# Attention with keys on partitions, no row maximum and v stationary, followed by the same SwiGLU with its weight tiles read again from DRAM

## The chip, the cores and the metric

One core of one Trainium2 chip runs the kernel. It has five engines with instruction queues of their own: TensorE (PE in the profile; its weight loads are listed as PEld), VectorE (DVE), ScalarE (ACT), GpSimd (POOL) and SyncE (SP), which here issues most DMAs. The metric is the device time of one execution in microseconds, lower is better. Three runs of the kernel before took 2514.51, 2516.18 and 2516.25 us; the median is 2516.18.

## The reference

Attention over 8 sequences and 12 heads, 448 tokens and 64 features a head, with q and k divided by their root mean square; then a SwiGLU block on the joined heads.

```
q, k, v: (8, 12, 448, 64) float32; g_q, g_k: (64,) float32
q_n, k_n = q / rms(q) * g_q, k / rms(k) * g_k      # rms over the 64 features
scores = q_n @ k_n^T / 8
attn   = exp(scores - max) / (sum(exp(scores - max)) + 1e-9)
x      = (attn @ v) as (3584 tokens, 768)
xn     = x / rms(x) * rms_g                        # over the 768 features
g, val = xn @ w_gate, xn @ w_val                   # 768 -> 1536
out    = (g * sigmoid(g) * val) @ w_out            # 1536 -> 768
```

The three weight matrices arrive as float64 and everything is computed in float32. The gains are `g = abs(randn(64)) + 0.5`; with the seed of the reference the largest absolute product g_q * g_k of one feature is 5.26. A vector of 64 features divided by its root mean square has length 8.

## The kernel before, in words

A sequence of 448 tokens is cut into four chunks of 112, and heads are taken in pairs: head 0 of a pair has its 64 features on partitions 0 to 63, head 1 on 64 to 127. There are 8 x 6 = 48 pairs, and the unit of attention is one chunk of 112 queries of one head, `(g, j, t)`: pair, head in the pair, chunk. There are 48 units a sequence.

For each pair, `norm_pair` (lines 132 to 149) divides q and k by their root mean square on GpSimd and VectorE, and `turn_pair` (lines 151 to 163) transposes both on TensorE so that features lie on partitions. `score` (L171) then gives 112 queries on partitions against all 448 keys; VectorE takes the row maximum (L173), ScalarE the exponential with the row sum (L175). `turn_e` (L181) transposes that tile in four pieces, copied out by VectorE and ScalarE in turn, because `values` (L194) needs keys on partitions: for each unit four matmuls with a transposed piece of e as the stationary operand and 64 columns of v streaming. After a pair the result is divided by the row sums (L204). Tokens lie on partitions, so after a sequence `norm_x` reduces along the row, and `turn_x` (L226) transposes x into `xT`, features on partitions.

The FFN of a sequence is 24 projections of six matmuls (`project`, L237; gate and value in turn over 12 blocks of 128 hidden features), a Tanh on ScalarE and two products on VectorE, which write `hT`; then eight output blocks of 112 tokens by 384 features, twelve matmuls each (`project_out`, L259). A float32 matmul is two passes, two MATMUL records in the trace.

The weights stay on chip as float32 for the whole kernel. `load_weight` (lines 86 to 110) reads a piece of float64 as pairs of 32-bit words and rounds it with four passes on VectorE, three on GpSimd and one on ScalarE. 60 pieces (36 of 512 columns, 24 of 384) are spread over the 48 units of the first sequence.

The order of work is written out in the loop at the end: at each unit a score, the weight pieces that are due, the transposes of the unit before, FFN items of the previous sequence in proportion to their cost, and the values of the unit before that. The first sequence has no FFN under it, and the FFN of the last has no attention over it. A scheduler arranges each engine's queue from this, so an engine's own order can differ a little from the program's.

Of the kernel before, what the change touches and what calls it, by code (L numbers as in the profile page):

```python
# [8 lines left out]
F32 = mybir.dt.float32  # L9
I32 = mybir.dt.int32  # L10
U32 = mybir.dt.uint32
I64 = mybir.dt.int64
ALU = mybir.AluOpType
ACT = mybir.ActivationFunctionType
AX_X = mybir.AxisListType.X
PSUM = bass.MemoryType.PSUM

B, H, S, D = 8, 12, 448, 64
DM, DF = H * D, 1536
NT, P = 4, 112  # a sequence is 4 chunks of 112 tokens; token p * 4 + t lies on partition p  # L20
# [3 lines left out]
CW = 512  # columns of a float64 weight chunk  # L24
# [3 lines left out]
def kernel(  # L28
# [12 lines left out]
):  # L41
    nc = tc.nc
# [41 lines left out]
    def load_weight(dst, src):  # L84
        """dst [128, n] float32; src [128, n] float32, or the bits of float64 as int64."""
# [15 lines left out]
        # 2^exponent with the sign, as float32 bits: 0 below float32's range, infinity above it.  # L101
# [4 lines left out]
        # The significand: its upper 21 bits exactly, then rounded with the lower 32.  # L106
# [25 lines left out]
    def norm_pair(g):  # L132
        """q and k over their root mean squares, as [token, (q k), chunk, head, d]."""
# [17 lines left out]
    def turn_pair(g):  # L151
        """Both transposed, d on partitions (64 for each head), times g_q / 8 and g_k."""
# [12 lines left out]
    def score(g, j, t):  # L165
        """Softmax numerators of 112 queries against all keys, and their sum."""
# [73 lines left out]
    def gate(b, fc):  # L240
        """2 * silu(g) = g * (1 + tanh(g / 2))"""
        project(b, fc, wg, "g")
        g = st.pop(("g", b, fc))
        th = th_pool.tile([128, S], F32, name="th")
        nc.scalar.activation(th, g, ACT.Tanh, scale=0.5)  # L245
        ga = st["ga", b, fc] = ga_pool.tile([128, S], F32, name="ga")
        nc.vector.scalar_tensor_tensor(ga, th, 1.0, g, ALU.add, ALU.mult)  # L247
# [78 lines left out]

# [28 lines left out]
```

## Time and profile before

| | |
|---|---|
| median of 3 runs | 2516.18 us (2514.51 to 2516.25) |
| profiled execution, span from first to last instruction | 2514.6 us |
| instructions | 24315 |
| TensorE matmul busy | 2406.5 us, 96% |
| TensorE weight loads | 1406.0 us, 56% |
| VectorE | 811.8 us, 32% |
| ScalarE | 532.8 us, 21% |
| GpSimd | 523.6 us, 21% |
| DMA | 73.92 MB, mean 29 GB/s |

The profiled execution is known by its span; the median of the timed runs is 1.6 us above it. Matmuls overlap in the array and the ends in their records are modelled, so the duration of a record is longer than the distance to the next start; weight loads run beside matmuls and are listed as an engine of their own. The page cuts the span into 40 slices of 63 us: in the first four TensorE is busy for 5 to 8 tenths, from the sixth on for 9 tenths and more in all but one, while VectorE and GpSimd have 5 to 8 tenths in the first four and 1 to 3 from the seventh on.

### The profile page before, as it was taken

What the parts mean: (1) busy time and instruction counts of PE and PEld (TensorE: products, weight loads), DVE (VectorE), ACT (ScalarE), POOL (GpSimd) and SP (SyncE); (2) the same over time, 40 slices, a digit from 0 to 9 for tenths busy, and PEclk for the clock granted to TensorE, in tenths of its full rate; (3) what the DMA queues carried; (4) which work ended last, traced back from release to release, by engine and by line L of the source; (5) the groups of instructions that cost most, each with busy time, mean ns of one, the idle gap of its engine ahead of it and who ended that gap; (6) DMA issues with size and microseconds to landing.
All of it is one profiled execution on the core that took longest, in us unless ns stands there. A gap on an engine that the chain in (4) does not pass through costs nothing.

```text
span 2514.6 us, 24315 instructions
## 1 busy us (share of the span) xinstructions
PE 2406.5 (96%) x9792; PEld 1406.0 (56%) x9792; DVE 811.8 (32%) x1337; ACT 532.8 (21%) x1285; POOL 523.6 (21%) x443
## 2 busy tenths in 40 slices
PE   5778899999999999999999999999999999999899
PEld 3445555555555555555555655555555565556455
DVE  5868733223322232222322233222332232221110
ACT  2223322212212122212212122222222122121100
POOL 7777612112111111111211211111121121110000
PEclk9999999999999999999999999999999999999999
DMA  4333200000000100000000000001000010000000
GB/s 125 123 119 108 85 12 19 15 22 24 18 15 17 30 21 11 19 26 22 19 12 14 28 25 15 12 25 32 11 19 15 22 30 12 8 6 11 6 1 22
DMA packets 48511, 73.92 MB, mean 29 GB/s; under 512 B 4880, under 2 KB 37136, under 8 KB 48400
## 3 DMA queue, kind: packets, MB, share of 16 engines
q1 hardware_dynamic: 47296, 72.37, 9.7%
q8 instruction: 78, 1.28, 0.2%
q14 instruction: 33, 0.27, 0.0%
q10 hardware_dynamic: 1104, 0.00, 0.0%
HBM read 61.35 MB, written 11.01 MB: 29 GB/s over the span
## 4 chain that ended last, share of the span: by engine, by line
PE 86%; POOL 6%; DVE 3%; issue 2%; ACT 2%; DMA 0%; POOLq 0%; ACTq 0%; SPq 0%; DVEq 0%
PE ff L237 35%; PE ff L259 20%; PE sc L171 12%; PE av L194 10%; PE tr L181 7%; PE tr L158 2%; PE tr L226 2%; POOL arena L103 1%; POOL arena L104 1%; ACT junk L214 1%; POOL rs L143 1%; DVE arena L109 1%; DVE arena L105 1%; POOL wg L110 1%; POOL qn L146 1%
## 5 line engine op out<-in xcount | busy, mean ns | idle before, releaser
L259 PE MATMUL ff<-wo,hT 128*112 128x384 f32 x1536 | 505.0, 486 | 0.0
L237 PE MATMUL ff<-xT,wg 128*128 128x448 f32 x1152 | 464.0, 549 | 0.0
L194 PEld LDWEIGHTS av<-vt,eT 112*112 112x112 f32 x3072 | 384.7, 194 | 133.5 <-issue 65.9
L237 PE MATMUL ff<-xT,wv 128*128 128x448 f32 x1152 | 452.5, 540 | 0.0
L171 PE MATMUL sc<-qkT 64*112 64x448 f32 x768 | 427.9, 646 | 8.8 <-ACT e L175 5.3
L194 PE MATMUL av<-vt,eT 112*112 112x64 f32 x3072 | 386.8, 275 | 26.3 <-DVE eT L184 12.7
L173 DVE TENSOR_REDUCE top<-sc 112x1 f32<-112x448 f32 x384 | 238.2, 622 | 483.7 <-PE sc L171 483.7
L137 POOL TENSOR_TENSOR qn<-qk 112x1024 f32<-112x1024 f32 x48 | 92.0, 1917 | 1424.1 <-issue 1313.0
L259 PEld LDWEIGHTS ff<-wo,hT 128*112 128x112 f32 x1536 | 267.2, 177 | 207.2 <-issue 0.4
L175 ACT ACTIVATE e<-sc,top 112x448 f32<-112x448 f32 x384 | 243.8, 635 | 500.9 <-DVE top L173 485.2
L237 PEld LDWEIGHTS ff<-xT,wv 128*128 128x128 f32 x1152 | 211.2, 190 | 177.6 <-issue 177.6
L237 PEld LDWEIGHTS ff<-xT,wg 128*128 128x128 f32 x1152 | 213.2, 193 | 171.7 <-issue 171.7
L181 PEld LDWEIGHTS tr<-ident,e 112*112 112x112 f32 x1536 | 164.6, 144 | 250.6 <-issue 149.8
L181 PE MATMUL tr<-ident,e 112*112 112x112 f32 x1536 | 246.7, 288 | 14.9 <-ACT e L175 14.9
L186 ACT COPY eT<-tr 112x448 f32<-112x448 f32 x192 | 101.9, 530 | 472.1 <-PE tr L181 472.1
L247 DVE SCALAR_TENSOR_TENSOR ga<-th,ff 128x448 f32<-128x448 f32 x96 | 59.6, 621 | 406.7 <-ACT th L245 406.7
L253 DVE SCALAR_TENSOR_TENSOR hT<-ga,ff 128x448 f32<-128x448 f32 x96 | 59.6, 621 | 337.4 <-PE ff L237 337.4
L171 PEld LDWEIGHTS sc<-qkT 64*112 64x112 f32 x768 | 113.1, 187 | 52.9 <-issue 18.9
L143 POOL TENSOR_TENSOR rs<-ms,mhalf 112x16 f32<-112x16 f32 x48 | 141.8, 2954 | 4.0
L245 ACT ACTIVATE th<-ff 128x448 f32<-128x448 f32 x96 | 52.1, 543 | 391.9 <-PE ff L237 391.9
L184 DVE COPY eT<-tr 112x448 f32<-112x448 f32 x192 | 118.2, 616 | 4.7 <-PE tr L181 4.3
L267 DVE COPY y<-ff 112x384 f32<-112x384 f32 x32 | 17.8, 558 | 272.6 <-PE ff L259 272.6
(40 smaller groups left out, 1021.5 us busy)
## 6 DMA issues: line engine op xcount, KB each, us to landing
qk<-in_q_dram SPq DMA_DIRECT2D x48, 224.0 KB, 2.9
qk<-in_k_dram SPq DMA_DIRECT2D x48, 224.0 KB, 3.2
vt<-in_v_dram SPq DMA_DIRECT2D x48, 224.0 KB, 2.6
out_dram<-y SPq DMA_DIRECT2D x32, 336.0 KB, 2.7
arena<-in_moe_w_gate_dram SPq DMA_DIRECT2D x18, 512.0 KB, 3.6
arena<-in_moe_w_val_dram SPq DMA_DIRECT2D x18, 512.0 KB, 3.6
arena<-in_moe_w_out_dram SPq DMA_DIRECT2D x24, 384.0 KB, 3.1
gq<-in_g_q_dram ACTq DMA_DIRECT2D x2, 0.2 KB, 3.3
```

The source lines that it names most:

```text
L137: nc.gpsimd.tensor_tensor(qn.rearrange("p a t h d -> p (a t h d)"), qk.rearrange("p a h x -> p (a h x)"), qk.rearrange("p a h x -> p (a h ...
L143: nc.gpsimd.tensor_tensor(rs, ms, mhalf[0:P, :], ALU.pow)
L171: nc.tensor.matmul(ps, lhsT=qkT[r, 0, t * P:(t + 1) * P], rhs=qkT[r, 1, :], start=True, stop=True)
L173: nc.vector.tensor_reduce(out=top, in_=ps, axis=AX_X, op=ALU.max, negate=True)
L175: nc.scalar.activation(e, ps, ACT.Exp, bias=top[:, 0:1], accum_out=st["den", g][:, j, t:t + 1])
L181: nc.tensor.transpose(ps[0:P, c, :], e[:, c * P:(c + 1) * P], ident[0:P, 0:P])
L184: nc.vector.tensor_copy(eT, ps[0:P])
L186: nc.scalar.copy(eT, ps[0:P])
L194: nc.tensor.matmul(av[:, j, t, :], lhsT=eT[:, c, :], rhs=vt[:, j, c, :], start=(c == 0), stop=(c == NT - 1))
L237: nc.tensor.matmul(ps, lhsT=w[:, c, fc * 128:(fc + 1) * 128], rhs=st["xT", b][:, c, :], start=(c == 0), stop=(c == NDC - 1))
L247: nc.vector.scalar_tensor_tensor(ga, th, 1.0, g, ALU.add, ALU.mult)
L259: nc.tensor.matmul(ps, lhsT=st["hT", b][:, fc, t * P:(t + 1) * P], rhs=wo[:, fc, n * HALF:(n + 1) * HALF], start=(fc == 0), stop=(fc == NF ...
```

## The change

The kernel before is kept whole as `any_scores`. A new program `safe_scores` comes first; it also sets a flag on the chip, and `any_scores` runs after it, behind a branch, where the flag is set. The flag is 8 times the largest absolute g_q * g_k against 80, the bound on a score from the lengths of the normed vectors.

In the new program the scores have keys on partitions: `score` takes a chunk of 112 keys as the stationary operand and streams all 448 queries. There is no maximum; the exponential takes the key's inverse root mean square as its per-partition scale, so k is transposed as it was loaded. The tile of exponentials can stream straight into `values`, where v is stationary (64 columns) and the result has features on partitions, head 0 on 0 to 63 and head 1 on 64 to 127. The sum over keys is six additions on GpSimd and one matmul per head with ones. x comes out as `xT`; its norm is a matmul with ones and one that spreads the result over partitions.

The weights of gate and value are held in three tiles of one block each. In the first FFN they are rounded from float64 and stored as float32 in DRAM; later sequences read them from there, three blocks ahead. `W_AHEAD` is that 3. `wo` stays on chip and is rounded block by block in the first FFN. Output blocks are 128 tokens instead of 112: six for an even sequence, whose last 64 tokens go with the next one's, and eight for an odd one. `fill` puts in FFN items of the sequence before; two of them (`LEFT`) are kept for the steps of the norm of x.

```
+    raw_pool, cv_pool = pool("c_raw", 2), pool("c_cv", 2)
...
+    nc.vector.tensor_scalar(flag, top, 8.0, SAFE, ALU.mult, ALU.is_gt)
...
+    def convert(dst, src):
+        if src.dtype == F32:
+            nc.sync.dma_start(out=dst, in_=src)
+            return
+        a, n = src.shape[1], src.shape[2]
+        assert a * n == DM
+        raw = raw_pool.tile([128, 2 * DM], I32, name="raw")
+        nc.sync.dma_start(out=raw.rearrange("p (a n w) -> p a (n w)", a=a, w=2).bitcast(I64), in_=src)
+        words = raw.rearrange("p (n w) -> p n w", w=2)
+        lo, hi = words[:, :, 0], words[:, :, 1]
+        top = cv_pool.tile([128, DM], I32, name="top")
+        nc.scalar.activation(top.bitcast(F32), hi.bitcast(F32), ACT.Abs)
+        nc.gpsimd.tensor_scalar(top.bitcast(F32), top.bitcast(F32), 122879.9921875, 2.0**-15, ALU.min, ALU.max)
+        nc.vector.tensor_scalar(top, top, 3, 0x3FFFFFF8, ALU.logical_shift_left, ALU.bitwise_and)
+        nc.vector.scalar_tensor_tensor(top, hi, -(2**30), top, ALU.bitwise_and, ALU.bitwise_or)
+        power = cv_pool.tile([128, DM], I32, name="power")
+        nc.vector.tensor_scalar(power, top, -(2**23), None, ALU.bitwise_and)
+        low = cv_pool.tile([128, DM], F32, name="low")
+        nc.vector.scalar_tensor_tensor(low, lo.bitcast(U32), 2.0**-52, power.bitcast(F32), ALU.mult, ALU.mult)
+        nc.gpsimd.tensor_tensor(dst.rearrange("p a n -> p (a n)"), top.bitcast(F32), low, ALU.add)
+    def weight(w, n):
...
+        if b == 0:
+            convert(t, src[:, fc * 128:(fc + 1) * 128].rearrange("(c p) f -> p c f", p=128))
+            nc.sync.dma_start(out=kept[w][fc], in_=t.rearrange("p c f -> p (c f)"))
+        else:
+            nc.sync.dma_start(out=t.rearrange("p c f -> p (c f)"), in_=kept[w][fc])
...
+    def score(g, cs):
+        for c in cs:
+            for j in range(2):
+                r = slice(j * D, (j + 1) * D)
+                ps = sc[c, j] = ps_s.tile([P, S], F32, name="sc")
+                nc.tensor.matmul(ps, lhsT=qkT[r, 1, c * P:(c + 1) * P], rhs=qkT[r, 0, :], start=True, stop=True)
+        for (c, j), ps in sc.items():
...
+            nc.scalar.activation(e, ps, ACT.Exp, scale=rs[:, n:n + 1])
+        for j in range(2):
...
+                    nc.gpsimd.tensor_tensor(es, es, st["e", g, c, j], ALU.add)
+    def values(g):
+        for c in range(NT):
+            for j in range(2):
+                nc.tensor.matmul(av[j * D:(j + 1) * D, 0:S], lhsT=vt[:, j, c, :], rhs=st["e", g, c, j],
+                                 start=(c == 0), stop=(c == NT - 1))
+        for j in range(2):
+            nc.tensor.matmul(den[j * D:(j + 1) * D, 0:S], lhsT=ones[0:P, :], rhs=st["es", g, j], start=True, stop=True)
...
+    def val(b, fc):
+        project(b, fc, "v")
...
+        weight("v", b * NFC + fc + W_AHEAD)
+        if b == 0:
+            weight_out(fc)
...
+    for g in range(NG):
...
+        load_pair(g + 2)
+        norm_pair(g + 1)
+        score(g, (0, 1))
+        fill()
+        score(g, (2, 3))
+        fill()
+        turn_pair(g + 1)
+        fill()
+        values(g)
+        divide(g)
+        fill()
+        if hp == NPAIR - 1:
+            fill(len(todo) - LEFT)
+            rms_x(b)
+            fill(1)
+            norm_x(b)
+            fill(1)
...
+    safe_scores(tc, *args, flag)
+    large = nc.values_load(flag[0:1, 0:1], min_val=0, max_val=1)
+    with tc.If(large > 0):
+        any_scores(tc, *args)
```

How the instructions of TensorE move in a steady stretch is seen from its queue. Before, inside the second sequence (`ff` are projections, `sc` scores, `tr` transposes, `av` values):

```order
L171 MATMUL sc<-qkT 112x448
L181 MATMUL tr<-ident,e 112x112 x4
L237 MATMUL ff<-xT,wg 128x448 x6
L194 MATMUL av<-vt,eT 112x64 x4
L171 MATMUL sc<-qkT 112x448
L181 MATMUL tr<-ident,e 112x112 x4
L194 MATMUL av<-vt,eT 112x64 x4
L171 MATMUL sc<-qkT 112x448
L181 MATMUL tr<-ident,e 112x112 x4
L237 MATMUL ff<-xT,wv 128x448 x6
```

After, at the same depth, with `den` the sums over keys:

```order
L500 MATMUL sc<-qkT 112x448 x4
L575 MATMUL ff<-xT,wg 128x448 x6
L500 MATMUL sc<-qkT 112x448 x4
L575 MATMUL ff<-xT,wv 128x448 x6
L575 MATMUL ff<-xT,wg 128x448 x6
L485 MATMUL tr<-ident,qn 128x112 x4
L485 MATMUL tr<-ident,qk 128x112 x4
L575 MATMUL ff<-xT,wv 128x448 x6
L520 MATMUL av<-e,vt 64x448 x8
L524 MATMUL den<-es,ones 64x448 x2
L575 MATMUL ff<-xT,wg 128x448 x6
```

Each short chain of value, score and transposes between two projections has given way to longer blocks, four scores or eight values and two sums at a time; the transposes left are those of q and k.

At the end of the first sequence TensorE's queue read before:

```order
L181 MATMUL tr<-ident,e 112x112 x4
L171 MATMUL sc<-qkT 112x448
L181 MATMUL tr<-ident,e 112x112 x4
L171 MATMUL sc<-qkT 112x448
L194 MATMUL av<-vt,eT 112x64 x8
L171 MATMUL sc<-qkT 112x448 x3
L226 MATMUL tr<-ident,x 128x112 x16
L237 MATMUL ff<-xT,wg 128x448
```

And now, with `msx` and `rb` the two small steps of the norm of x:

```order
L500 MATMUL sc<-qkT 112x448 x8
L485 MATMUL tr<-ident,qn 128x112 x4
L485 MATMUL tr<-ident,qk 128x112 x4
L520 MATMUL av<-e,vt 64x448 x8
L524 MATMUL den<-es,ones 64x448 x2
L500 MATMUL sc<-qkT 112x448 x8
L555 MATMUL msx<-ones,ss 112x1 x4
L565 MATMUL rb<-ident,rs_789 128x112 x4
L485 MATMUL tr<-ident,qn 128x112 x4
L575 MATMUL ff<-xT,wg 128x448 x6
```

The transposes of x between the first projections are gone; scores of the next pair stand ahead of the norm, and a whole pair's work has no projection in it.

VectorE's queue holds the rounding of weights. In the first sequence before (`arena` are its pieces):

```order
L105 SCALAR_TENSOR_TENSOR arena<-arena 128x512
L109 SCALAR_TENSOR_TENSOR arena<-arena 128x512
L102 TENSOR_SCALAR arena<-arena 128x512
L107 TENSOR_SCALAR arena<-arena 128x512
L184 COPY eT<-tr 112x448
L173 TENSOR_REDUCE top<-sc 112x1
L105 SCALAR_TENSOR_TENSOR arena<-arena 128x512
L109 SCALAR_TENSOR_TENSOR arena<-arena 128x512
```

And in the second sequence now, where `ga` and `hT` are the gating products of the FFN:

```order
L417 SCALAR_TENSOR_TENSOR top<-raw,top 128x768
L420 TENSOR_SCALAR power<-top 128x768
L422 SCALAR_TENSOR_TENSOR low<-raw,power 128x768
L590 SCALAR_TENSOR_TENSOR hT<-ga,ff 128x448
L416 TENSOR_SCALAR top<-top 128x768
L417 SCALAR_TENSOR_TENSOR top<-raw,top 128x768
L420 TENSOR_SCALAR power<-top 128x768
L422 SCALAR_TENSOR_TENSOR low<-raw,power 128x768
L584 SCALAR_TENSOR_TENSOR ga<-th,ff 128x448
L490 COPY qkT<-tr 128x448
```

The rounding stood between the maxima and copies of attention; it now stands between the two products that the projections' PSUM banks wait for.

## Rows read from the trace of the kernel before

**Rows 1.** The page's engine line (busy us, share, instructions) and chain by line.
```profile
PE 2406.5 (96%) x9792; PEld 1406.0 (56%) x9792; DVE 811.8 (32%) x1337; ACT 532.8 (21%) x1285; POOL 523.6 (21%) x443
...
PE ff L237 35%; PE ff L259 20%; PE sc L171 12%; PE av L194 10%; PE tr L181 7%; PE tr L158 2%; PE tr L226 2%; POOL arena L103 1%; POOL arena L104 1%; ACT junk L214 1%; POOL rs L143 1%; DVE arena L109 1%; DVE arena L105 1%; POOL wg L110 1%; POOL qn L146 1%
```

**Rows 2.** Timeline of TensorE, steady stretch: start us, us, engine, line, operation, tiles.
```profile
...
1509.55 0.91 PE L194 MATMUL av<-vt,eT 112*112 112x64 f32 x8
1510.39 1.00 PE L171 MATMUL sc<-qkT 64*112 64x448 f32 x2
1511.32 0.59 PE L181 MATMUL tr<-ident,e 112*112 112x112 f32 x4
1511.75 0.91 PE L194 MATMUL av<-vt,eT 112*112 112x64 f32 x8
1512.59 1.00 PE L171 MATMUL sc<-qkT 64*112 64x448 f32 x2
...
```

**Rows 3.** The chain in order of time: start us, us, what; the FFN.
```profile
499.07 7.74 PE ff L259 x24
...
2340.85 107.50 PE ff L237 x286
2448.36 61.93 PE ff L259 x192
```

**Rows 4.** Stretches: length, busy per engine, granted clock, DMA share, GB/s; start, seam, inside.
```profile
20.00:310.00 290.00, 228.33 (x762) 141.20 (x763) 219.34 (x344) 88.68 (x201) 222.70 (x214) 1.00 0.37 110
597.00:608.00 11.00, 9.15 (x41) 5.10 (x41) 5.85 (x11) 6.42 (x16) 1.21 (x2) 0.78 0.08 22
620.00:880.00 260.00, 260.00 (x1098) 151.14 (x1098) 70.44 (x118) 50.78 (x126) 41.12 (x30) 1.00 0.07 20
```

**Rows 5.** Timeline of TensorE in the first sequence, columns as in rows 2.
```profile
36.65 1.62 PE L194 MATMUL av<-vt,eT 112*112 112x64 f32 x8
38.19 1.83 PE L171 MATMUL sc<-qkT 64*112 64x448 f32 x2
```

**Rows 6.** Timeline of TensorE at two seams: two adjacent scores of different heads.
```profile
598.43 1.34 PE L171 MATMUL sc<-qkT 64*112 64x448 f32 x4
...
2042.96 1.34 PE L171 MATMUL sc<-qkT 64*112 64x448 f32 x4
```

**Rows 7.** Groups by line (busy us, mean ns, idle before): normalization and exponentials.
```profile
L175 ACT ACTIVATE e<-sc,top 112x448 f32<-112x448 f32 x384 | 243.8, 635 | 500.9 <-DVE top L173 485.2 <-PE tr L181 15.4
L143 POOL TENSOR_TENSOR rs<-ms,mhalf 112x16 f32<-112x16 f32 x48 | 141.8, 2954 | 4.0
L146 POOL TENSOR_TENSOR qn<-qk,rs 112x512 f32<-112x512 f32 x96 | 98.1, 1042 | 3.8
L137 POOL TENSOR_TENSOR qn<-qk 112x1024 f32<-112x1024 f32 x48 | 92.0, 1917 | 1424.1 <-issue 1313.0 <-PE tr L158 107.5 <-DMA qk<-in_k_dram 3.6
```

**Rows 8.** Groups by line: VectorE's passes of a weight conversion, 512 columns wide.
```profile
L105 DVE SCALAR_TENSOR_TENSOR arena<-arena 128x512 int32<-128x512 int32 x36 | 41.3, 1149 | 47.6 <-POOL arena L104 46.9
L109 DVE SCALAR_TENSOR_TENSOR arena<-arena 128x512 f32<-128x512 uint32 x36 | 26.1, 726 | 0.0
L107 DVE TENSOR_SCALAR arena<-arena 128x512 int32<-128x512 int32 x36 | 24.6, 683 | 0.0
L102 DVE TENSOR_SCALAR arena<-arena 128x512 int32<-128x512 int32 x36 | 18.5, 515 | 8.0 <-DMA arena<-in_moe_w_gate_dram 6.1 <-POOL wv L110 1.9
```

**Rows 9.** The page's DMA issues: KB each, median us from issue to landing.
```profile
arena<-in_moe_w_gate_dram SPq DMA_DIRECT2D x18, 512.0 KB, 3.6
arena<-in_moe_w_out_dram SPq DMA_DIRECT2D x24, 384.0 KB, 3.1
```

**Rows 10.** Timeline at the start: first work on q and k, first score.
```profile
4.95 1.89 POOL L137 TENSOR_TENSOR qn<-qk 112x1024 f32<-112x1024 f32 x1 [3.65 <-DMA qk<-in_k_dram]
...
25.54 3.29 PE L171 MATMUL sc<-qkT 64*112 64x448 f32 x4 [3.48 <-DVE qkT L163]
```

More of the change, by code (lines that the diff above doesn't have):

```diff
@@ L16 @@
 PSUM = bass.MemoryType.PSUM
+DRAM = bass.MemoryType.DRAM
 B, H, S, D = 8, 12, 448, 64
@@ L24, with any_scores @@
 CW = 512
+SAFE = 80.0
 @with_exitstack
-def kernel(
+def any_scores(
     ctx: ExitStack,
@@ L328, with kernel @@
+@with_exitstack
+def kernel(ctx: ExitStack, tc: tile.TileContext, *args):
+    nc = tc.nc
+    flag = ctx.enter_context(tc.tile_pool(name="flag", bufs=1)).tile([1, 1], I32, name="flag")
+    safe_scores(tc, *args, flag)
+    large = nc.values_load(flag[0:1, 0:1], min_val=0, max_val=1)
+    with tc.If(large > 0):
+        any_scores(tc, *args)
 _INS = ["q", "k", "v", "g_q", "g_k", "moe_w_gate", "moe_w_val", "moe_w_out", "moe_rms_g"]
```

227 lines of the change are left out of this document (added).

## The prediction

> **What bounds the kernel now.** I read the page's engine line and its chain first, then a piece of the steady stretch instruction by instruction, then the start, and last the side engines. TensorE is busy 96% of the span, and the chain of waits runs 35% through the gate and value projections, 20% through the output projection, 12% through scores, 10% through `av` and 7% through the transposes of e [rows 1]. Everything else is cover, so the steady stretch has to be priced in TensorE time, by the distance from one start to the next and not by busy means, because the records overlap.
>
> One unit (112 queries of one head) in the steady stretch: `av` 1509.55 to 1510.39 is 0.84 us, scores to 1511.32 are 0.93, the four transposes of e to 1511.75 are 0.43; from one score to the next it is 2.20 us [rows 2]. A projection of a sequence's 24 blocks is 107.5 us (286 of its 288 passes are in the row, so one pass of 448 columns is 0.376 us), an output block of 24 passes 7.74 us [rows 3]. A sequence before: 48 x 2.20 = 105.6, turning q and k 6 x 2 x 0.43 = 5.2, projections 107.5, eight output blocks 61.9, turning x about 24 x 0.11 = 2.6: 282.8 us. The period, read from two seams five sequences apart, is (2042.96 - 598.43)/5 = 288.9 us [rows 6]; the other 6 us are the seam, where the granted clock averages 0.78 against 1.00 inside a sequence [rows 4].
>
> The first 320 us are another regime. There `av` takes 1.62 us where it later takes 0.91, a score 1.83 where it later takes 1.00 [rows 5, 2]: these are the durations of the 1.2 GHz level, although the clock column prints 1.00 for that stretch, so I go by the durations. TensorE is busy only 228 of 290 us there, VectorE 219 and GpSimd 223 [rows 4]: the float64 weights are being rounded, and attention of the first sequence waits in the same queues.
>
> **Part by part.**
>
> Scores. Still eight matmuls of two passes per pair of heads, but now heads alternate within a group of four. Two adjacent scores of different heads (the 99th and 100th unit counted from 0: last chunk of head 0, first of head 1, so rows 0 to 63 and 64 to 127 of the array) took 1.34 us together, against 1.00 for a single one [rows 6, 2]; the second began 0.33 us into the first, when its score bank came free. So row halves overlap. A group of four then costs four passes, 1.50 us, plus 0.18 for entering and leaving (0.93 less two passes) and 0.1 for the stagger: 1.8 us, 3.6 a pair. Serial it would be 6.4.
>
> Values and denominators. All 32 short `av` matmuls and 32 transposes of a pair go; eight matmuls of 448 columns come, and two more for the sum over keys. They alternate between output partitions 0 to 63 and 64 to 127. No row of before shows column halves. The bounds: side by side like the row halves, ten passes, 3.76 us; one after the other, twenty passes, 7.5 us. I take side by side, by the nearest row (the 1.34 us), with 0.3 for mode changes: 4.0. The Trainium skill, "TensorE: Matmul & The Clock Gate", Part 3 (Measured speedup), gives 2.38 times for three column tiles; at that efficiency an estimate is 4.7 us instead of 3.76, some 45 us over the kernel. "TensorEngine Tiling (Array Packing)", Key Properties, of the same skill speaks against the change: changing the tiling mode drains the engine. The trace agrees: the 0.18 us round each score above is that drain; but the change goes from eight such blocks a pair to three.
>
> With 0.86 for the eight transposes of q and k, a pair costs 3.6 + 4.0 + 0.9 = 8.5 us, against 8 x 2.20 + 0.86 = 18.5 before.
>
> FFN. Projections stay: 8 x 107.5 = 860. Output blocks are now 128 tokens, so six and eight alternate: 56 x 7.74 = 433.4 instead of 495. Turning x goes; eight small matmuls replace it (about 2 us a seam), and two output blocks (15 us) are held back to lie over the square root and the scaling, so I charge no clock drop at the seams.
>
> First sequence. q lands at about 4.95 us [rows 10]. Then Square (1.1), the sum on VectorE (1.2), the power and the multiply on GpSimd (0.3 + 2.95 + 1.04) [rows 7], transposes and copy (1.7): the first score at about 14 us, where before it was 25.5 [rows 10]. Then six pairs with no FFN under them. I take the 1.2 GHz level, since attention alone never left it before: twice 8.5, 17 us a pair, 102 us. GpSimd's share of a pair is seven sums at about 0.84 (1917 ns for 1024 columns, scaled [rows 7]), the power and the multiply: 10.2 us, below 17; exps are 8 x 0.64 = 5.1 on ScalarE. The seam has no cover here: 10 us. Together, with a slow start of the first projections, 130 us.
>
> Weights. Six conversions are done in the first sequence, thirty fall under the second. What they do is nearly the same, one GpSimd pass less, but before they were spread over 60 pieces in about 310 us: 27,648 columns, 8.6 us per 768. VectorE alone needs 1.15 + 0.73 + 0.68 + 0.52 = 3.07 us per 512 [rows 8], 4.6 per 768: these are the two ends. Behind each conversion on VectorE queue the gating products that free the two `ff` banks, and on SP the loads of q and k; so a late conversion holds TensorE. I take 7.0, nearer the slow end since only two raw buffers of 768 KB stand where three of 512 KB did, each landing in 3.6 us before [rows 9]: 30 x 7.0 = 210, then the output blocks and the attention left, 62. The second sequence ends 272 after its start instead of 207: +65 (4.6 gives 0, 8.6 gives +113).
>
> Re-reading 9.4 MB a sequence is 45 GB/s over some 210 us; the start moved 110 GB/s [rows 4]. Its loads are asked for three blocks (27 us and more) ahead and land in a few us. I cost this at nothing; were the cover gone, each load would cost its landing, 24 x 3.6 = 86 us a sequence.
>
> End. The last copy, its store, a flag load and a branch over the general program: 7 us (0 to 15; the store's share is in the 4 us after the last pass before).
>
> Sum: 130 + 860 + 433.4 + 42 x 8.5 (357) + 7 x 2 + 65 + 7 = 1866 us of span. The profiled span before, 2514.6, is 1.6 below the median of the runs, so I predict 1868.
>
> **Rivals.**
>
> A: column halves run one after the other. For it: no row shows them, and both halves stream from the same partitions, unlike the row halves. Against it: the row halves do overlap in float32. 42 x 3.75 = 157, and 45 in the slow first sequence: 2070.
>
> B: rounding paces the second sequence harder, because two raw buffers serve where three did: 8.6 x 3/2 = 12.9 per conversion, 30 x 12.9 + 62 = 449, 242 over 207, in place of the 65: 2045. For it: SP's order now puts the store of each finished block, which waits for GpSimd, ahead of the next raw load. Against it: the start before kept 110 GB/s with attention in the same queues.
>
> C: the first sequence runs at 2.4 GHz and the conversions are hidden: 130 becomes 95, 65 becomes 0: 1768.
>
> D, slower than before: TensorE falls to the 1.2 GHz level inside the sequences. The first 320 us before show that a busy share of 79% does not lift it when the work is attention [rows 4, 5], and the new half-array blocks could keep it down. The seven steady sequences, 7 x (107.5 + 2) + 371 of output blocks + 357 = 1495 us, would cost that again: 3363. It decides from 650 us of full-speed work run at half rate, 43% of the steady stretch. Against it: before, with 39% of a sequence in attention, the level stayed at 1.00 between seams [rows 4], and now attention is 24%.
>
> E: the change does not do what it says. If the flag were set, the general program would follow: 1868 + 2515. The flag compares 8 times the largest product of g_q and g_k with 80; for the seeded inputs it is 8 x 5.26 = 42. And should not even the row halves overlap in these groups, 42 x 2.8 + 17 on top of A: 2205.
>
> **How the numbers follow.** Forecast 0.60, A 0.17, B 0.10, C 0.08, D 0.03, E 0.02 (all of it for the second form). The likeliest case alone runs from 1800 to 1945 (conversions 0 to +113, the first sequence -35, the end, 0.3 us a pair either way). To leave out less than 2 in 10 the range must take in A and B: 1785 to 2080. Below it lies half of C, above it some of A and B, D and E: 0.15. A difference below 0.2%, 5 us, is what a measurement cannot tell from none. Every case but D is far on the faster side: faster 0.97, same 0.005, slower 0.025.
>
> **What would show it.** In the profile after: a group of four scores in about 1.8 us and a pair's `av` and `den` in about 4.0; were it 7.5, A holds. Starts of the first projections at about 130 us. In the second sequence TensorE waits for weight tiles from GpSimd or for `hT` and `ga` on VectorE, some 65 us in all, and none in the third to eighth, whose period should be near 207 to 222 us. The granted clock at 1.00 without dips at the seams. The forecast is wrong if TensorE waits in the third sequence or later, or if the start takes over 180 us.

## The result, and the profile after

The changed kernel takes 1902.76 us, the median of four runs (1901.21 to 1904.55), against 2516.14 us for the kernel before on the same chip: a ratio of 0.756, 95% interval 0.755 to 0.757. The forecast was 1868, 34.8 us too low. The profiled execution has a span of 1900.4 us.

The starts of the first projection of each sequence's FFN cut both traces into comparable pieces. Before they lie at 320.0, 608.8 and so on to 2337.9 us, after at 153.6, 427.3, 651.9, 860.2, 1084.7, 1293.0, 1517.6 and 1723.4.

| piece | before | after | forecast |
|---|---|---|---|
| start to the first projection | 320.0 | 153.6 | 130 |
| second sequence (FFN of the first under it) | 288.8 | 273.7 | 272 |
| third to eighth, six periods | 1729.1 | 1296.1 | 1287 |
| last FFN and the end | 176.7 | 177.0 | 176 |

So 433 of the 614 us come from the steady stretch, 166 from the start, 15 from the second sequence. The periods are now 224.5 and 208.3 us in turn (the last 205.8), for 288.9 before. Where the forecast misses, it misses at the start: 24 of its 35 us.

The page's engine lines of the kernel after, with TensorE's busy tenths and granted clock in 40 slices of 47.5 us (answering to [rows 1]):

```profile
PE 1788.5 (94%) x5888; PEld 880.5 (46%) x5888; DVE 577.8 (30%) x618; ACT 412.7 (22%) x689; POOL 687.4 (36%) x563
...
PE   4768777899999999999999999999999999999998
...
PEclk9788888999999999999999999999999999999999
```

TensorE has 5888 matmul records for 9792. From the ninth slice (380 us) to the last but one it is busy for nine tenths and more, and its clock is at nine tenths and more from the eighth. What is lost lies in the first eight slices. The same in windows (columns as in [rows 4]): the start, the second sequence, two steady periods and the last FFN.

```profile
16.00:153.00 137.00, 90.76 (x299) 36.10 (x300) 68.71 (x59) 50.78 (x83) 106.53 (x84) 0.78 0.34 99
153.00:427.00 274.00, 229.19 (x704) 109.91 (x702) 174.32 (x176) 67.02 (x102) 154.94 (x113) 0.90 0.40 128
...
652.00:860.00 208.00, 208.00 (x712) 102.23 (x712) 52.66 (x58) 47.05 (x81) 72.03 (x61) 1.00 0.25 71
860.00:1085.00 225.00, 225.00 (x763) 112.30 (x762) 53.30 (x59) 48.56 (x84) 71.23 (x60) 1.00 0.24 68
1723.00:1894.00 171.00, 170.69 (x482) 91.20 (x480) 17.36 (x29) 8.43 (x16) 0.00 (x0) 1.00 0.17 51
```

The first number after the length is TensorE's busy time: 208.00 of 208 and 225.00 of 225 in the steady periods, so TensorE waits for nothing there. In the second sequence 45 of 274 us are missing, at a mean clock of 0.90; at the start 46 of 137, at 0.78. The dips to 0.78 between sequences [rows 4] are gone: the steady periods show 1.00, seams included.

TensorE in the steady stretch of the kernel after (columns as in [rows 2]); each distance is read from one start to the next:

```profile
703.99 3.23 PE L520 MATMUL av<-e,vt 112*64 112x448 f32 x16
707.05 0.92 PE L524 MATMUL den<-es,ones 112*64 112x448 f32 x4
707.90 4.78 PE L575 MATMUL ff<-xT,wv 128*128 128x448 f32 x12
712.61 1.76 PE L500 MATMUL sc<-qkT 64*112 64x448 f32 x8
714.29 4.78 PE L575 MATMUL ff<-xT,wg 128*128 128x448 f32 x12
```

Values and denominators take 703.99 to 707.90, 3.91 us for twenty passes (forecast 4.0; 7.5 if the column halves ran one after the other). Four scores take 712.61 to 714.29, 1.68 us for eight passes (forecast 1.8). That is the time of ten passes and of four, at 0.375 a pass, plus 0.16 and 0.18. A pair with its eight transposes costs some 8.1 us where it cost 18.5.

The side engines, groups by line of the kernel after (busy us, mean ns | idle before, what ended it); the first two answer to nothing of before and the forecast had to estimate them or missed them:

```profile
L512 POOL TENSOR_TENSOR es<-es,e 112x448 f32<-112x448 f32 x192 | 223.3, 1190 | 153.4 <-ACT e L504 153.3
...
L532 DVE RECIPROCAL rd<-den 128x448 f32<-128x448 f32 x48 | 141.9, 2955 | 107.1 <-PE den L524 107.1
...
L417 DVE SCALAR_TENSOR_TENSOR top<-raw,top 128x768 int32<-128x768 int32 x36 | 48.2, 1340 | 0.9
L416 DVE TENSOR_SCALAR top<-top 128x768 int32<-128x768 int32 x36 | 39.8, 1107 | 85.1 <-POOL top L414 85.0
```

A sum over keys costs GpSimd 1.19 us in the mean (1.13 in the steady stretch), not 0.84. A reciprocal of 448 columns costs VectorE 2.96 us, 6.6 ns a column. The last row shows how the rounding spends its time: of 85.1 us that VectorE stood idle ahead of its first pass, 85.0 ended with GpSimd's clamp (L414). The means of L416 and L417 hold waits as well; the experiments come back to them.

### The profile page after: what moved, and what is told of

Read it like the earlier page. It is cut to its first block, busy times and chain, and to the rows that moved or that the text cites. A ratio compares the mean times of both kernels' runs of the same rounds, so it can differ in the third digit from the quotient of the medians.

```text
span 1900.4 us, 15809 instructions
## 1 busy us (share of the span) xinstructions
PE 1788.5 (94%) x5888; PEld 880.5 (46%) x5888; DVE 577.8 (30%) x618; ACT 412.7 (22%) x689; POOL 687.4 (36%) x563
## 5 line engine op out<-in xcount | busy, mean ns | idle before, releaser
L600 PE MATMUL ff<-wo,hT 128*128 128x384 f32 x1344 | 444.9, 489 | 0.0
L600 PEld LDWEIGHTS ff<-wo,hT 128*128 128x128 f32 x1344 | 251.5, 190 | 182.6 <-issue 17.6
L512 POOL TENSOR_TENSOR es<-es,e 112x448 f32<-112x448 f32 x192 | 223.3, 1190 | 153.4 <-ACT e L504 153.3
L504 ACT ACTIVATE e<-sc,rs 112x448 f32<-112x448 f32 x384 | 212.4, 635 | 210.4 <-PE sc L500 210.4
L508 POOL TENSOR_TENSOR es<-e 112x448 f32<-112x448 f32 x96 | 109.8, 1163 | 266.0 <-ACT e L504 266.0
L500 PE MATMUL sc<-qkT 64*112 64x448 f32 x768 | 184.7, 578 | 9.4 <-ACT e L504 8.5
L520 PE MATMUL av<-e,vt 112*64 112x448 f32 x768 | 165.8, 577 | 10.0 <-ACT qkT L488 6.1
L532 DVE RECIPROCAL rd<-den 128x448 f32<-128x448 f32 x48 | 141.9, 2955 | 107.1 <-PE den L524 107.1
L520 PEld LDWEIGHTS av<-e,vt 112*64 112x64 f32 x768 | 53.5, 144 | 111.8 <-issue 98.1
L471 POOL TENSOR_TENSOR qn<-qk,rs 112x512 f32<-112x512 f32 x48 | 50.7, 1057 | 96.8 <-PE tr L485 96.4
```

The costliest lines, as they stand in the source:

```text
L500: nc.tensor.matmul(ps, lhsT=qkT[r, 1, c * P:(c + 1) * P], rhs=qkT[r, 0, :], start=True, stop=True)
L504: nc.scalar.activation(e, ps, ACT.Exp, scale=rs[:, n:n + 1])
L508: nc.gpsimd.tensor_tensor(es, st["e", g, 0, j], st["e", g, 1, j], ALU.add)
L512: nc.gpsimd.tensor_tensor(es, es, st["e", g, c, j], ALU.add)
L520: nc.tensor.matmul(av[j * D:(j + 1) * D, 0:S], lhsT=vt[:, j, c, :], rhs=st["e", g, c, j], start=(c == 0), stop=(c == NT - 1))
L532: nc.vector.reciprocal(rd, den[:, 0:S])
```

## Experiments

Each kernel is timed in three rounds beside the kernel before, the last one in five; medians are given, and differences against the changed kernel's 1902.8.

**Does order decide the overlap of the column halves?** Heads one after the other in `values`, instead of in turn:

```
-        for c in range(NT):
-            for j in range(2):
+        for j in range(2):
+            for c in range(NT):
                 nc.tensor.matmul(av[j * D:(j + 1) * D, 0:S], lhsT=vt[:, j, c, :], rhs=st["e", g, c, j],
```

> The changed kernel with the eight value matmuls of a pair in another order: the four of head 0 (columns 0 to 63 of the array), then the four of head 1. Same work, same instructions. If column halves overlap only where they alternate in TensorE's queue, a pair's values go from eight passes side by side to about sixteen one after the other, 3.0 us more a pair: 42 x 3.0 = 126 in the steady part, little of it hidden in the first sequence, so 2030 us (2015 to 2050). If TensorE picks matmuls of a free half out of its queue whatever their order, under 10 us more: 1903 to 1913. If the halves never overlapped, no change.

1957.81 us (1956.05 to 1959.50): +55, between the two expectations. The periods grow to 233.8 and 217.7 us, 9.3 each, 1.55 a pair. TensorE of this kernel in stretches: to 717.7 us, from 718.1 to 719.3, two lines from 719.3 to 720.2, and the end of the block:

```profile
716.23 1.72 PE L520 MATMUL av<-e,vt 112*64 112x448 f32 x4
...
717.78 1.72 PE L520 MATMUL av<-e,vt 112*64 112x448 f32 x8
...
719.35 0.59 PE L524 MATMUL den<-es,ones 112*64 112x448 f32 x1
719.72 0.54 PE L520 MATMUL av<-e,vt 112*64 112x448 f32 x1
...
720.84 0.92 PE L524 MATMUL den<-es,ones 112*64 112x448 f32 x2
721.69 2.52 PE L575 MATMUL ff<-xT,wv 128*128 128x448 f32 x6
```

In the first 1.5 us four passes start, in the next 1.5 us eight; the block lasts 716.23 to 721.69, 5.46 us instead of 3.91. All eight passes of head 0 stand ahead of head 1's in the program. The trace doesn't name the head of a pass, but the starts fall into two chains with a step of 0.375 us each: the second chain begins at 717.79, 6 ns after the first one's fifth pass, while the first one's eighth starts at 718.91. The sums do the same: the first `den` pass starts at 719.35, 6 ns after the fifth pass of the second chain, with three `av` passes still to come. So TensorE takes a pass for a free half of the array ahead of waiting ones, but here not ahead of eight: four passes of 0.375 us, 1.5 us a pair, are what the order in the program is worth. This takes the queue to have the program's order within the block, which the trace doesn't print. The Trainium skill, "TensorE: Matmul & The Clock Gate", Part 3 (What overlaps and what doesn't), holds that matmuls start and end strictly in program order; by that head 1's first pass could start no earlier than head 0's eighth, at 718.91, and the trace, which has it 1.12 us earlier, disagrees. What sets the four was not sought.

**The same for the row halves of the scores.**

```
-        for c in cs:
-            for j in range(2):
+        for j in range(2):
+            for c in cs:
                 r = slice(j * D, (j + 1) * D)
```

> The changed kernel with each group of four scores ordered by head (two on rows 0 to 63, then two on rows 64 to 127) instead of alternating. If order decides, the second half starts when the first half's last pass has been issued, about 1.1 us late: 84 groups x 1.1 = 92 us, 1995 us (1970 to 2010). If the queue looks past the waiting passes, no change: 1903 within 8.

1905.77 us (1902.29 to 1906.62): no difference that can be told. TensorE of this kernel:

```profile
714.40 1.77 PE L500 MATMUL sc<-qkT 64*112 64x448 f32 x8
716.10 4.78 PE L575 MATMUL ff<-xT,wg 128*128 128x448 f32 x12
```

1.70 us against 1.68: with only four passes a head ahead, the order costs nothing, which fits what the first run showed.

**What does rounding cost in all?** The seven passes of `convert` are replaced by one copy of the upper words, its loads and stores stay:

```
-        nc.scalar.activation(top.bitcast(F32), hi.bitcast(F32), ACT.Abs)
...
-        nc.gpsimd.tensor_tensor(dst.rearrange("p a n -> p (a n)"), top.bitcast(F32), low, ALU.add)
+        nc.scalar.copy(dst.rearrange("p a n -> p (a n)"), hi.bitcast(F32))
```

> The changed kernel with the rounding of float64 left out: the raw bytes are still read, and one ScalarE copy of the upper words (wrong numbers) takes the place of four VectorE, two GpSimd and one ScalarE pass. If the rounding passes stretch the first sequence and the second, the second falls from 274 to about 208 and the first projection starts at 135 to 145 instead of 154: 1903 - 66 - 12 = 1825 us (1805 to 1845). If the landing of the raw bytes sets the pace (two raw buffers), less than 25 us is gained: 1878 to 1903.

1818.69 us (1817.24 to 1819.86): -84. Its windows, the start and the second sequence:

```profile
16.00:136.00 120.00, 85.25 (x299) 33.57 (x300) 33.07 (x27) 48.40 (x81) 82.15 (x70) 0.82 0.34 99
136.00:345.00 209.00, 208.72 (x704) 102.55 (x702) 55.78 (x64) 68.36 (x105) 65.39 (x55) 0.99 0.56 175
```

The second sequence is 208.4 us long, like the steady ones: rounding adds 65.3 there, and 17 at the start (136.6 for 153.6). The loads alone, at 175 GB/s, don't hold TensorE (208.72 us busy of 209).

**Are GpSimd's sums what stretches the start?** Head 1's sums go to VectorE in the first sequence:

```
-                nc.gpsimd.tensor_tensor(es, st["e", g, 0, j], st["e", g, 1, j], ALU.add)
+                add = nc.vector if g < NPAIR and j == 1 else nc.gpsimd
+                add.tensor_tensor(es, st["e", g, 0, j], st["e", g, 1, j], ALU.add)
...
-                    nc.gpsimd.tensor_tensor(es, es, st["e", g, c, j], ALU.add)
+                    add.tensor_tensor(es, es, st["e", g, c, j], ALU.add)
```

> The changed kernel with head 1's sums over keys moved from GpSimd to VectorE in the first sequence only (18 additions of 112x448). If GpSimd's queue stretches the pairs of the first sequence, six pairs lose 2 to 4 us each: 1885 us (1878 to 1893). If the clock level or the chain through TensorE sets them, no change within 4 us. If VectorE's queue (rounding and the 2.95 us reciprocal) is the longer one, it gets slower by 5 to 15 us.

1884.62 us (1883.97 to 1886.17): -18, as expected. The first projection comes at 136.0, the second sequence is unchanged (273.0). The first `den` of the six pairs starts at 34.7, 52.2, 69.5, 88.6, 104.4 and 117.6 us; in the changed kernel at 32.9, 55.2, 75.7, 99.5, 117.0 and 131.6. Over the first three steps, in which rounding shares the queue, a pair takes 20 to 24 us with all sums on GpSimd and 17 to 19 with them split; the forecast had 17.

**Do the two buffers for raw weights pace the second sequence?** A third one:

```
-    raw_pool, cv_pool = pool("c_raw", 2), pool("c_cv", 2)
+    raw_pool, cv_pool = pool("c_raw", 3), pool("c_cv", 2)
```

> The changed kernel with three raw buffers for the float64 bytes instead of two, nothing else. If the time that a raw buffer is held (landing 4.4 us, then the passes that read it) paces the second sequence at 7.2 us per conversion, three buffers bring it towards the VectorE sum of 4.6: 30 x 1.5 = 45 us less, 1858 us (1845 to 1875). If the queues of VectorE and GpSimd pace it, no change: within 5 us of 1903.

1908.70 us (1908.30 to 1910.08): no gain, 6 us the other way. What ScalarE's first pass waits for in the second sequence (us in total, times, longest), in the changed kernel:

```profile
ACT top L413 <- DMA raw<-in_moe_w_val_dram: 43.3, 8, 8.7
ACT top L413 <- DMA raw<-in_moe_w_out_dram: 36.9, 10, 7.6
ACT top L413 <- DMA raw<-in_moe_w_gate_dram: 27.0, 5, 6.9
```

and with the third buffer:

```profile
ACT top L413 <- POOL wg L423: 51.9, 9, 9.4
ACT top L413 <- POOL wo L423: 38.0, 9, 8.7
ACT top L413 <- POOL wv L423: 28.8, 8, 5.5
```

107 us of waiting for a landing have become 119 us of waiting for GpSimd's last pass, which frees `top`. The wait that ended with a DMA looked like the bound; without it another of the same size stood in its place.

**And the buffers behind it?** Three of `raw` and of `top`, with one for `power` to make room:

```
+    raw_pool, cv_pool = pool("c_raw", 3), pool("c_cv", 2)
+        top = cv_pool.tile([128, DM], I32, name="top", bufs=3)
+        power = cv_pool.tile([128, DM], I32, name="power", bufs=1)
```

> Three raw buffers alone moved the waits in the second sequence from the raw bytes to the rounding's first scratch tile (top, two buffers, held until GpSimd's last pass). Here both have three buffers. If buffers pace the rounding, now neither does: 7.2 us per conversion falls towards 5.5, the second sequence from 274 to about 235: 1865 us (1850 to 1880). If the in-order queues of ScalarE, GpSimd and VectorE pace it, no gain: 1898 to 1912.

1903.42 us (1902.85 to 1904.05): the same. Its second sequence is 277.1 us long, VectorE 198 busy of 277:

```profile
151.00:428.00 277.00, 228.17 (x701) 109.23 (x701) 198.47 (x173) 65.67 (x101) 162.88 (x112) 0.89 0.39 123
```

These two lists of buffers don't pace the rounding; `low` (two buffers) and the weight tiles (three) stayed as they were. Left is the way of a conversion itself, through ScalarE, GpSimd, VectorE and GpSimd again, each a queue in order with attention and gating in it.

**Fewer crossings.** The clamp moves from GpSimd to VectorE, where the next passes run:

```
-        nc.gpsimd.tensor_scalar(top.bitcast(F32), top.bitcast(F32), 122879.9921875, 2.0**-15, ALU.min, ALU.max)
+        nc.vector.tensor_scalar(top.bitcast(F32), top.bitcast(F32), 122879.9921875, 2.0**-15, ALU.min, ALU.max)
```

> The changed kernel with the rounding's min and max pass on VectorE instead of GpSimd, which takes one crossing between the two queues out of each conversion. If the crossings pace it (VectorE waits 85 us for that pass in the first two sequences), 36 x 1 to 1.5 us: 1855 us (1845 to 1880). If VectorE's own work paces it (174 of 274 us busy, and 0.6 us more per conversion), 1903 to 1920.

1894.43 us (1887.99 to 1895.69): -8, between the two. The second sequence falls from 273.7 to 264.1, the start gets 3 us longer. So the clamp's place costs something, about a seventh of the 65. The run doesn't separate the crossing from the time that the clamp takes on GpSimd, and VectorE, 198 busy of 273, isn't full either.

What the traces show besides is that the passes of the two engines hold each other up. In the second sequence of the changed kernel the same pass of VectorE (L416) takes 501 to 3248 ns, while the products that write `hT` take 605 to 616:

```profile
L416 DVE TENSOR_SCALAR top<-top x28: 501/561/3248, 164.1 to 360.0; 128x768 int32<-128x768 int32 x28
...
L590 DVE SCALAR_TENSOR_TENSOR hT<-ga,ff x12: 605/612/616, 168.6 to 367.6; 128x448 f32<-128x448 f32 x12
```

(The three figures are the shortest, the median and the longest in ns.) GpSimd and VectorE at one long pass of L416, and at a short one:

```profile
198.32 1.80 POOL L423 TENSOR_TENSOR wg<-top,low 128x768 f32<-128x768 f32 x1
...
198.38 2.15 DVE L416 TENSOR_SCALAR top<-top 128x768 int32<-128x768 int32 x1 [3.30 <-POOL top L414]
...
213.09 0.55 DVE L416 TENSOR_SCALAR top<-top 128x768 int32<-128x768 int32 x1
```

VectorE's pass starts 0.06 us after GpSimd's addition and ends 0.41 us after its end. Of the 112 rounding passes on VectorE in this sequence, 43 start while GpSimd is in a clamp, an addition or a product, and together they take 39 us longer than such passes take alone (0.56 us for L416 and L420, 0.96 for L417 and L422). The other 69 lose nothing, also those that start under GpSimd's power of 2.91 us. So 39 of VectorE's 124 us of rounding are spent behind GpSimd's passes. With three of `raw` and `top` it is 66 us, which fits that these buffers gain nothing, and with the clamp on VectorE 49. No run keeps these passes apart, so how much of the 65 us it accounts for stays open.

**Is the re-read hidden?** Every gate and value load is issued a second time, into a tile that nobody reads:

```
+            again = w_pool.tile([128, DM], F32, name="again", bufs=2)
+            nc.sync.dma_start(out=again, in_=kept[w][fc])
```

> The changed kernel with every weight tile read from DRAM a second time into a tile that nothing uses (168 more loads of 384 KB, 9.4 MB more a sequence). The prediction costed the re-read at nothing; if that is right, doubling it changes nothing: 1903 within 6 us, steady periods of 224.5 and 208.3 stay. If the loads are near the limit of the queue or of the DMA engines, each extra one shows up to its landing of 3.0 us: up to 168 x 3.0 = 504 us more.

1938.09 us (1935.95 to 1942.24): +35, but the run doesn't test what it was meant to. Held by no reader, the extra loads ran ahead: the last was issued at 643 us, and 105 of the 168 were issued in the third sequence, the only steady period that grew (224.5 to 260.5). Its loads, and its window:

```profile
again<-kept_v SPq DMA_DIRECT2D x53, 384.0 KB, 3.8
again<-kept_g SPq DMA_DIRECT2D x52, 384.0 KB, 3.9
...
```

The window of that sequence:

```profile
425.00:686.00 261.00, 232.89 (x763) 115.41 (x762) 52.57 (x59) 47.76 (x85) 71.25 (x60) 0.94 0.72 219
```

At 219 GB/s, with the DMA engines busy 72%, the loads of q and k come late (ScalarE waits 88 us for them here), and TensorE stands 28 us. So there is a point at which re-reading would cost, but it lies above the 68 GB/s of a steady period.

**The same, tied to its block.** The gate tile is doubled and the second load goes into its other half, so it can't start before its block is free (`power` has one buffer here, for room):

```
+        more = 2 if w == "g" else 1
+        t2 = w_pool.tile([128, more * NDC, 128], F32, name=f"w{w}", tag=f"w{w}")
+        t = st["w", w, n] = t2[:, 0:NDC, :]
...
+            if w == "g":
+                nc.sync.dma_start(out=t2[:, NDC:2 * NDC, :].rearrange("p c f -> p (c f)"), in_=kept[w][fc])
```

> In the kernel that reads every tile twice the 168 extra loads were not spread: nothing in the program held them, so they ran ahead into one stretch. Here the extra load (gate tiles only, 84 of 384 KB) goes into the second half of the tile that the block uses, so each waits for TensorE to leave that buffer, as its twin does; the scratch tile of the rounding's power goes from two buffers to one to make room. If re-reading is hidden, the periods of the later sequences stay at 224.5 and 208.3: 1903 within 6 us. If the loads are near a limit, 84 x up to 3.0 us: up to 250 us more.

1903.94 us (1902.41 to 1906.06): no difference, with the period from 860 us at 89 GB/s instead of 68:

```profile
860.00:1085.00 225.00, 225.00 (x763) 112.29 (x764) 53.65 (x60) 47.93 (x82) 71.22 (x60) 1.00 0.29 89
```

TensorE is busy without a gap here as well. The re-read is hidden, and so is half as much again.

**What does the branch cost?** The flag's load, the branch and the general program behind it are left out:

```
-    large = nc.values_load(flag[0:1, 0:1], min_val=0, max_val=1)
-    with tc.If(large > 0):
-        any_scores(tc, *args)
```

> The changed kernel without the flag load, the branch and the general program behind it. The prediction gave the whole end 7 us and measured 6.7 from the last pass to the end of the span, where the kernel before had 4.3: so 2 to 4 us less, 1899 to 1901. If the longer program also costs at the start or in instruction loading along the way, more: 5 to 15 us less.

1900.16 us (1899.33 to 1901.28): -2.6, near what a measurement can tell; the general program costs little or nothing where it isn't taken.

**What is the row maximum worth by itself?** The kernel before, without it:

```
-        top = small.tile([P, 1], F32, name="top")
-        nc.vector.tensor_reduce(out=top, in_=ps, axis=AX_X, op=ALU.max, negate=True)
-        nc.scalar.activation(e, ps, ACT.Exp, bias=top[:, 0:1], accum_out=st["den", g][:, j, t:t + 1])
+        nc.scalar.activation(e, ps, ACT.Exp, accum_out=st["den", g][:, j, t:t + 1])
```

> The kernel before with one part of the change alone: no row maximum (384 VectorE reductions of 622 ns go, the exponential follows the scores at once). If TensorE bounds the steady part, only the first 320 us gain, where VectorE was busy 76% of the time: 10 to 25 us less, 2500 us (2488 to 2512). If the maximum sat on a chain that TensorE waits for, up to 48 x 0.4 us a sequence: 100 us or more less.

2495.23 us (2494.31 to 2497.13), a ratio of 0.992 to the kernel before: -21. The first projection comes 38 us earlier (281.7), and what follows gives 16 back: 10 in the second sequence (298.7 for 288.8) and 6 in the six periods after it (1735.2 for 1729.1). Why was not sought. Of the 613 us, then, some 21 come from leaving out the maximum alone. The rest comes with the other parts of the change, the layout of attention and the output blocks of 128 tokens among them, which no run separates.

**The two gains together.** Head 1's sums on VectorE in the first sequence, and the clamp on VectorE for the thirty conversions after the first six:

```
+        st["n"] = st.get("n", 0) + 1
+        clamp = nc.gpsimd if st["n"] <= 2 * W_AHEAD else nc.vector
+        clamp.tensor_scalar(top.bitcast(F32), top.bitcast(F32), 122879.9921875, 2.0**-15, ALU.min, ALU.max)
...
+                add = nc.vector if g < NPAIR and j == 1 else nc.gpsimd
```

> Both changes that paid, together: head 1's sums on VectorE in the first sequence, and the min and max pass on VectorE for the 30 conversions of the second sequence (the first six stay on GpSimd). If the two act in different sequences, as the traces of the two runs say, the gains add: 18 and 10 us, 1875 us (1870 to 1880). If the earlier start only moves the rounding against the same queues, the second gain is lost: 1885.

1870.09 us (1868.88 to 1875.95, five runs), a ratio of 0.744 to the kernel before (0.743 to 0.745): -33 against the changed kernel, and the fastest version with all of the computation. Its start and second sequence:

```profile
16.00:131.00 115.00, 78.02 (x298) 32.43 (x299) 83.46 (x79) 50.74 (x83) 89.94 (x64) 0.83 0.40 117
131.00:395.00 264.00, 222.59 (x704) 106.91 (x702) 197.14 (x204) 66.87 (x102) 140.06 (x85) 0.92 0.42 132
```

The first projection starts at 131.6 us, 22 earlier; the second sequence is 263.5 long, 10 shorter. The kernel without rounding is 51 us faster, and that is all in the second sequence (208.4 us there).

## Why the prediction was right, and where a term was mis-sized

The mechanism held where most of the time is: fewer, longer matmuls in two halves of the array at once, and a steady stretch bound by TensorE alone. That the second sequence is stretched by rounding held too. At the start the forecast had the wrong engine as the slowest. The terms:

- **Column halves (no row of before showed them).** Taken as side by side from the row halves [rows 6]: 3.91 us for 4.0. The Trainium skill's 2.38 times for three column tiles ("TensorE: Matmul & The Clock Gate", Part 3) would have given 4.7 by the prediction's estimate; two halves of 64 columns lost nothing beyond 0.16 us a block. Rival A is out. But the overlap owes part of itself to the program's order, on which the prediction put no price: heads one after the other cost 55 us.
- **Steady periods.** Forecast 222 and 207, measured 224.5 and 208.3. The distances in the period from 652 us show what cancels: attention came out cheaper (scores 1.68 for 1.8 a group, values 3.91 for 4.0), while the projections take 111.1 us for 107.5. The last FFN, with no attention over it, has 108.2 by the same reading, so some 2.9 us stand at the 18 half-array blocks of the period. The change of mode is paid on both sides of a block, and the forecast charged it on one.
- **Start, +24: the step that was mis-sized.** The prediction had 14 to the first score, 17 a pair and 10 for the seam; the first score came at 15.9, and from there to the last `den` it took 116 us instead of 102. The 17 assumed that TensorE at 1.2 GHz is the slowest, with GpSimd at 10.2 a pair beside it. GpSimd's sums were scaled from a product of 1024 columns [rows 7] to 0.84 us and take 1.13 where nothing disturbs them, 1.28 in the mean of the first sequence; with the power and the product a pair is some 12 us, and the two conversions that fall on each of the first three pairs bring 2 x (0.83 + 1.9) for their two GpSimd passes. That is 17 to 18 us of work in one in-order queue, and pairs of 20 to 24 us. TensorE's first scores in the kernel after, GpSimd and TensorE in the fourth pair, and TensorE at the seam, with the first projection in the last line (in brackets the wait before, and what ended it):

```profile
15.86 4.94 PE L500 MATMUL sc<-qkT 64*112 64x448 f32 x12 [0.81 <-DVE qkT L490]
...
98.01 3.24 POOL L512 TENSOR_TENSOR es<-es,e 112x448 f32<-112x448 f32 x2
...
99.50 3.54 PE L524 MATMUL den<-es,ones 112*64 112x448 f32 x4 [4.55 <-POOL es L512]
...
147.77 1.65 PE L555 MATMUL msx<-ones,ss 128*112 128x1 f32 x8 [7.32 <-POOL ss L543]
...
153.60 6.70 PE L575 MATMUL ff<-xT,wg 128*128 128x448 f32 x12
```

  TensorE stands 4.55 us until a sum is done. The run with split sums takes 18 us off and confirms it. The seam was 22 us from the last `den` instead of 10: a reciprocal of 2.96 us and a GpSimd sum stand in its chain (the `msx` row: 7.32 us of waiting for the sum of squares), which the forecast had not listed.
- **Conversions, +65: the size right by luck, the reason not.** The second sequence is 273.7 for 272, and the kernel without rounding shows 65.3 us. The thirty conversions end one each 7.2 us. But the forecast chose 7.0, between ends of 4.6 and 8.6, because two raw buffers stood for three, and three buffers, with or without a third `top`, gain nothing. Its lower end was a sum of means too [rows 8]; alone, the four VectorE passes of 768 columns take 3.0 us now. What the runs show in place of the buffers is a way over three in-order queues, of which the clamp's move gave back 10 us, and 39 us of VectorE's passes behind GpSimd's; the split of the 65 between them stays open. Of the 65 us TensorE stands idle for 45, and 20 are work at a lower clock (busy 229 us for 209 without rounding). The largest of the 45 are two waits that the forecast named, in us, times and the longest:

```profile
PE ff L575 <- DVE hT L590: 15.3, 5, 5.7
...
PE ff L575 <- DVE ga L584: 9.8, 2, 5.6
```

  Rival B, raw buffers as the pace, falls with the same two runs; rival C would have needed hidden conversions.
- **Clock.** No seam dips, as forecast; up to TensorE's last pass, all of the granted clock below 1.00 lies before 362 us (columns as in [rows 4]):

```profile
362.00:1894.00 1532.00, 1531.12 (x5117) 767.62 (x5116) 352.00 (x399) 299.74 (x516) 441.39 (x374) 1.00 0.22 65
```

  In the first sequence the level changed, 0.78 in the mean, and TensorE stood 46 of 137 us, where the forecast had it at work at 1.2 GHz throughout. Rival D fails: half-array blocks, a fifth of the steady stretch, leave the clock at 1.00.
- **Re-read, costed at nothing:** confirmed by the run tied to its block. **End:** 6.7 us for 7. **Rival E:** no instruction of the general program in the trace, and both kinds of halves overlap.

## What to carry to other kernels

Two half-array matmuls side by side took half the time in float32 too (twenty passes in the time of ten), with the program naming them in turn; count passes, not matmuls, and add the change of mode on both sides of the block. Where several engines hand one item round, as in the rounding here, a longer list of buffers can merely move the wait; look at which queue is in order, what else stands in it, and whether one engine's pass takes longer while another works. Compare the shortest and the median duration of a pass before taking its mean as a price, and price each side engine's operation from a row of the same kind and width before calling it covered. A second read from DRAM beside a TensorE-bound stretch cost nothing here at 68 and 89 GB/s; it cost where the loads that set the next work, here q and k, no longer landed in time.

## What the runs showed that was not expected

- A float32 reciprocal on VectorE takes 2955 ns for 448 columns where a product of the same width takes 620 (group `hT`): almost five times as long.
- GpSimd adds two 112x448 float32 tiles in some 1130 ns in the steady stretch, 2.5 ns a column (1163 to 1190 in the mean of the kernel); the row that it was scaled from had 1.9 [rows 7].
- A rounding pass on VectorE that starts while GpSimd is in a clamp, an addition or a product ends after GpSimd's pass: 39 us in the second sequence of the changed kernel.
- TensorE takes matmuls for the free half of the array past four waiting passes, not past eight (5.46 us against 3.91).
- The clock column of the kernel before printed 1.00 over a start whose durations were those of the 1.2 GHz level [rows 4, 5]; without the row maximum the same stretch prints 0.70, of which the part from 20 to 100 us prints 1.00 and that from 140 to 260 us 0.50:

```profile
20.00:310.00 290.00, 242.01 (x894) 159.00 (x895) 206.64 (x302) 89.91 (x216) 221.13 (x215) 0.70 0.37 110
```

  Durations are the safer reading there.
